# Position bias by a float16 compare on VectorE, sums written by head, placing and high parts on ScalarE

## The chip, the cores and the metric

One core of one Trainium2 chip runs the whole program. The metric is the device time of one execution in microseconds (us). The engines are TensorE (PE; PEld is its weight load), VectorE (DVE), ScalarE (ACT), GpSimd (POOL) and SyncE (SP), whose queue issues nearly all DMAs.

## The reference

The program is an attention with a position bias that a small network computes, then a dense mixture in float64 weights, then a routed one. The change is in the bias and in how float64 weights are converted.

```python
pos = np.arange(S)                      # S = 576
psi_rel = np.log1p(np.abs(pos[:, None] - pos[None, :]))
psi_i = np.log1p(np.maximum(pos[:, None], 1.0))
x = (psi_rel / psi_i)[..., None]
h = np.maximum(x @ w1 + b1, 0.0)        # 32 hidden units
bias = h @ w2                           # 8 heads
scores = q @ k^T / 8 + bias             # then softmax, @ v
...
a, b = x @ moe_w1, x @ moe_w2           # x: [2304, 512]
x = (a * b @ moe_w3) @ moe_w_out
...
out = second mixture: one of 8 experts per row
```

The bias of a query i and a distance d is piecewise linear: unit h counts where w1 log1p(d) + b1 log1p(i) is positive. So for each distance and unit there is a mask over the queries, and the bias is a product of masks with coefficients.

## The kernel before, in words

`build` runs four parts: `p0` (position bias, and the product w3 @ w_out that folds two weights into one), `p1` (attention), `p2` (first mixture), `p3` (second mixture). The order of the instructions on each engine is the order in which the program is written.

`p0` goes through nine groups `gg` of 64 distances. 128 partitions hold 4 distances times 32 units, so a group has 16 masks of up to 576 queries (L239 to L250; the last three groups need 512, 384 and 256 columns only, by `COLS`). For each of up to five query tiles `t` of 128 (or 64) queries, TensorE multiplies each mask by three bfloat16 parts of the coefficients `mv` (L324): 48 products of 64 columns into one PSUM tile `pb`, of which there are three. 39 such tiles are made in all. The 64 columns hold two sums, one that is divided by log1p(i) and one that is not, for 4 distances and 8 heads. `evac` then has ScalarE scale the first sum into `tmp` (L255) and VectorE add the second, writing the distance table `ds` (L266). `flush` writes a finished table of 128 distances to `dsym` in DRAM (L208) and, mirrored by POOL into buffers `md` (L222), a second time (L225). There are two `md` buffers, which the pieces of w3 @ w_out use as well (L236, L237).

Coefficients: POOL multiplies and splits them into three parts `p3a` (L142, L144, L155), and VectorE places them with four instructions, one for each distance of the four, zeros elsewhere (`place`, L151). The constant sum's parts `p3c` are placed once for each of two buffers.

Masks of the next group are made while a group's products run. `NACT` says how many of 16 ScalarE makes, as a steep sigmoid (L248); the others VectorE makes with a compare (L250).

Woven in are 24 conversions of float64 weights (`conv_steps`, L79): the high word is scaled (L93 or, on ScalarE, L91; `CVE` names the engine of each), three VectorE steps put in the low bits (L97, L98, L99), POOL makes the high part in TensorE's rounded format (L193) and subtracts it to give the low part (L194). SP loads the next piece (L169) when a piece has been converted. `mixed` is the list in which a group's masks on VectorE, conversion steps and placing are sorted by their place in the group; it is cut into as many pieces as there are tiles, and after each piece stands the add of the tile before.

`p2_operands` converts 16 pieces of the first mixture's weights with the same steps, the scaling on VectorE (`mul`, L642), then a cast to the high part on ScalarE (L661) and POOL's subtraction (L659).

## Time and profile before

| | |
|---|---|
| Time, median of 3 runs | 1084.18 us (1083.52 to 1087.68) |
| Span of the profiled execution, first to last instruction | 1082.5 us |
| Busy share of the span | PE 93%, PEld 83%, DVE 74%, ACT 63%, POOL 41% |
| First product of the attention's scores | 157.09 us |
| Busy from 0 to 157 us | PE 105.98, DVE 138.76, ACT 101.83, POOL 107.57 us |

The profile shows one execution of the program. The span is the time from its first to its last instruction; the runs' times include what lies around it. A busy share is an average over parts with different limits, so the stretch in which a change lies is read by itself. DVE, ACT, POOL, PE, SP are the engines' names in the rows; L12 is line 12 of the kernel before; `a<-b,c` says which tile is written and which are read.

### The profile page before, as it was taken

What the parts mean: (1) busy time and instruction counts of PE and PEld (TensorE: products, weight loads), DVE (VectorE), ACT (ScalarE), POOL (GpSimd) and SP (SyncE); (2) the same over time, 40 slices, a digit from 0 to 9 for tenths busy, and PEclk for the clock granted to TensorE, in tenths of its full rate; (3) what the DMA queues carried; (4) which work ended last, traced back from release to release, by engine and by line L of the source; (5) the groups of instructions that cost most, each with busy time, mean ns of one, the idle gap of its engine ahead of it and who ended that gap; (6) DMA issues with size and microseconds to landing.
All of it is one profiled execution on the core that took longest, in us unless ns stands there. A gap on an engine that the chain in (4) does not pass through costs nothing.

```text
span 1082.5 us, 21989 instructions
## 1 busy us (share of the span) xinstructions
PE 1005.4 (93%) x8118; PEld 898.7 (83%) x8118; DVE 799.3 (74%) x1447; ACT 677.5 (63%) x1263; POOL 442.2 (41%) x503
## 2 busy tenths in 40 slices
PE   4587789999999999989999999999979999999995
PEld 3566677888888888789999999999978888888884
DVE  8987988999999999999612221222487999989995
ACT  7766556898989888734422222222125888888884
POOL 5766857888888878445300000000033112111220
PEclk9899999999999999989999999999989999999998
DMA  5689765533353432144010000000223326411273
GB/s 170 148 220 240 181 200 163 162 117 109 116 167 112 120 104 83 58 137 146 31 40 10 11 21 21 21 10 11 105 108 120 115 68 213 156 40 40 71 251 96
DMA packets 62419, 116.69 MB, mean 108 GB/s; under 512 B 14495, under 2 KB 33439, under 8 KB 62048
## 3 DMA queue, kind: packets, MB, share of 16 engines
q1 hardware_dynamic: 58496, 104.14, 31.4%
q0 software_dynamic: 3520, 10.75, 3.0%
q8 instruction: 67, 1.10, 0.4%
q14 instruction: 48, 0.39, 0.1%
q10 hardware_dynamic: 288, 0.30, 0.1%
HBM read 155.83 MB, written 25.15 MB: 167 GB/s over the span
## 4 chain that ended last, share of the span: by engine, by line
PE 49%; issue 15%; DMA 11%; DVE 8%; ACT 1%; POOL 0%; POOLq 0%; DVEq 0%; ACTq 0%
PE ab L694 15%; DMA out<-or,sci 10%; PE sc L463 8%; PE o L763 8%; PE pv L549 6%; PE tr L500 5%; PE pv L544 3%; DMA raw<-in_w 1%; PE pv L493 1%; DVE cva L98 1%; PE pv L232 1%; DVE cva L99 1%; DVE cva L97 1%; DVE t L470 1%; DVE cva L93 1%
## 5 line engine op out<-in xcount | busy, mean ns | idle before, releaser
L489 POOL TENSOR_SCALAR e<-e,su 128x576 f32<-128x576 f32 x144 | 114.9, 802 | 58.4 <-DVE su L485 44.8
L740 DVE TENSOR_TENSOR g<-ab,asb 128x256 f32<-128x256 f32 x72 | 30.4, 422 | 143.3 <-ACT asb L739 143.1
L470 DVE CUSTOM_DVE_ANT_0 t<-sc,nb 128x576 f32<-128x576 f32 x144 | 108.4, 753 | 14.4 <-PE sc L463 11.7
L479 ACT ACTIVATE e<-t,mn 128x576 f32<-128x576 f32 x144 | 112.2, 779 | 6.6 <-DVE mn L470 5.1
L324 PE MATMUL pb<-mv,mask 128*128 128x64 bf16 (+1 forms) x1872 | 70.9, 202 | 42.1 <-DVE ds L266 30.5
L1310 POOL DMA_INDIRECT out<-or,sci x21 | 24.8, 1181 | 204.5 <-ACT or L1309 194.8
L324 PEld LDWEIGHTS <-mask 128*128 128x128 bf16 (+1 forms) x1872 | 66.8, 107 | 50.0 <-issue 41.6
L530 DVE TENSOR_TENSOR etl<-tr,eth 128x512 fp32r<-128x512 f32 x144 | 98.5, 684 | 7.4 <-ACT eth L521 4.3
L463 PE MATMUL sc<-kh,qs 128*128 128x288 f32 x320 | 97.6, 322 | 4.5 <-DVE ds L266 4.5
L521 ACT CAST eth<-tr 128x512 fp32r<-128x512 f32 x144 | 83.7, 582 | 28.4 <-PE tr L500 26.3
L935 POOL DMA_INDIRECT xh<-x2r,gi x1 | 1.4, 1354 | 243.8 <-DMA w1r<-in_w1e 243.8
L1207 DVE TENSOR_TENSOR w1l<-w1r,w1h 128x1024 fp32r<-128x1024 f32 x80 | 92.6, 1221 | 5.1 <-ACT w1h L1206 5.1
L694 PE MATMUL ab<-xh,wh 128*128 128x256 f32 x576 | 94.8, 287 | 0.5 <-DVE g L740 0.5
L1258 DVE TENSOR_TENSOR w2l<-w2r,w2h 128x1024 fp32r<-128x1024 f32 x80 | 92.6, 1220 | 2.7
L694 PE MATMUL ab<-xh,wl 128*128 128x256 f32 x576 | 93.5, 285 | 0.4 <-POOL wl L659 0.4
L694 PE MATMUL ab<-xl,wh 128*128 128x256 f32 x576 | 93.4, 285 | 0.0
L463 PE MATMUL sc<-kl,qs 128*128 128x288 f32 x320 | 89.8, 296 | 0.0
L500 PE MATMUL tr<-k_ident,e 128*128 128x128 f32 x576 | 86.4, 273 | 3.1 <-DVE etl L530 3.1
L463 PEld LDWEIGHTS sc<-kh,qs 128*128 128x128 f32 x320 | 60.6, 189 | 30.9 <-issue 11.6
L1206 ACT CAST w1h<-w1r 128x1024 fp32r<-128x1024 f32 x84 | 82.1, 1069 | 0.0
L694 PEld LDWEIGHTS ab<-xh,wh 128*128 128x128 f32 x576 | 80.0, 193 | 1.1 <-DVE g L740 0.8
L694 PEld LDWEIGHTS ab<-xh,wl 128*128 128x128 f32 x576 | 80.2, 193 | 0.6 <-POOL wl L659 0.6
(304 smaller groups left out, 2864.9 us busy)
## 6 DMA issues: line engine op xcount, KB each, us to landing
w1r<-in_w1e SPq DMA_DIRECT2D x84, 512.0 KB
w2r<-in_w2e SPq DMA_DIRECT2D x80, 512.0 KB
q<-in_qd SPq DMA_DIRECT2D x16, 576.0 KB
k<-in_kd SPq DMA_DIRECT2D x16, 576.0 KB
w<-in_w3t SPq DMA_DIRECT2D x16, 512.0 KB
raw<-in_w SPq DMA_DIRECT2D x16, 512.0 KB
nb<-dsym SPq DMA_DIRECT2D x7, 1152.0 KB
dsym<-ds SPq DMA_DIRECT2D x14, 512.0 KB
```

What stands on the lines that cost most here:

```text
L324: nc.tensor.matmul(out=pb[:n, s], lhsT=m_[:, s % 8, P * t:P * t + n], rhs=mv[:, k, s], start=(k == 0), stop=(k == 2))
L463: nc.tensor.matmul(out=sc[:, f, 0:288], lhsT=l, rhs=r, start=(n == 0), stop=(n == len(lst) - 1))
L470: nc.vector.tensor_tensor_reduce(out=t_.rearrange("p (f k) -> p f k", f=2), in0=sc[:, :, 0:288], in1=pre.nb[h % 2][:, tt, :].rearrange("p ...
L479: nc.scalar.activation(out=e, in_=t_, func=AF.Exp, scale=-1.0, bias=mn, accum_out=su[:, i % 2:i % 2 + 1])
L489: nc.gpsimd.tensor_scalar(out=e, in0=e, scalar1=su[:, i % 2:i % 2 + 1], scalar2=1.0, op0=ALU.mult, op1=ALU.mult)
L500: nc.tensor.transpose(pt[:, kb, :], e[:, P * kb:P * kb + P], ident)
L521: nc.scalar.copy(out=dh, in_=src)
L530: nc.vector.tensor_tensor(out=dl, in0=src, in1=dh.bitcast(F32), op=ALU.subtract)
L694: nc.tensor.matmul(out=p[:, a], lhsT=w[f][:, a, k, :], rhs=x[:, k, :], start=(k == 0 and n == 0), stop=(k == KD - 1 and n == 2))
L763: nc.tensor.matmul(out=o[:, a, 0:c1 - c0], lhsT=g[:, sl], rhs=w[:, f, c0:c1], start=(f == 0 and n == 0), stop=(f == KF - 1 and n == 2))
L1207: eng.tensor_tensor(out=w1l[:, k], in0=w1r[:, k], in1=w1h[:, k].bitcast(F32), op=ALU.subtract)
L1258: nc.vector.tensor_tensor(out=w2l[:, sl], in0=w2r[:, sl], in1=w2h[:, sl].bitcast(F32), op=ALU.subtract)
```

## The change

Masks: all 144 are made on VectorE by one compare. Its input is no longer a float32 row of -b1 log1p(i) but the query's number itself in float16 (`qi`), times the sign `sg` of -b1, and the threshold is, for each distance and unit, sg times (exp(w1 log1p(d) / -b1) - 1), made once at the start by short operations and one exponential on ScalarE. `NACT`, the steep sigmoid and ScalarE's masks go.

Sums: `mv` and `pb` are laid out by head, so that `ds` gets runs of 32 distances of one head (forward for query tiles 0 and 1, backward for 2 to 4) in place of single words 128 apart. A mask product now writes its 64 columns in runs of 4 words.

Placing (`place`) goes from VectorE to ScalarE, all first scalings of conversions go to ScalarE (6 of `p0`'s 24 and all 16 of `p2`'s were elsewhere), and `p0`'s high parts go from POOL to ScalarE. At the start, both placings and all 16 masks of the first group come one after the other.

```diff
@@ conv_steps
-            if eng == "A":
-                nc.scalar.activation(out=f, in_=src, func=AF.Copy, scale=2.0 ** -112)
-            else:
-                (nc.vector if eng == "V" else nc.gpsimd).tensor_scalar(out=f, in0=src, scalar1=2.0 ** -112, scalar2=1.0, op0=ALU.mult, op1=ALU.mult)
+            lambda: nc.scalar.activation(out=f, in_=hi.bitcast(F32), func=AF.Copy, scale=2.0 ** -112),
@@ p0
-            nbP = T(c, [P, S], F32, "nbP")
+            qi = T(c, [P, S], F16, "qi")
-            mvs = [T(c, [P, 3, 16, 2, 4, H], BF16, f"mv{r}") for r in range(2)]
+            mvs = [T(c, [P, 3, 16, 2, H, 4], BF16, f"mv{r}") for r in range(2)]
-            v.tensor_scalar(out=nbP, in0=nbP, scalar1=b1c, scalar2=-1.0, op0=ALU.mult, op1=ALU.mult)
-            v.tensor_scalar(out=wL, in0=L4, scalar1=w1c, scalar2=None, op0=ALU.mult)
-            v.tensor_scalar(out=wS, in0=wL, scalar1=STEEP, scalar2=None, op0=ALU.mult)
+            v.tensor_scalar(out=nb, in0=b1c, scalar1=-1.0, scalar2=None, op0=ALU.mult)
...
+            v.tensor_scalar(out=th, in0=L4, scalar1=rb, scalar2=7.0, op0=ALU.mult, op1=ALU.min)
+            v.tensor_scalar(out=qi, in0=qi, scalar1=sg, scalar2=None, op0=ALU.mult)
+            v.tensor_scalar(out=th, in0=th, scalar1=-80.0, scalar2=None, op0=ALU.max)
+            nc.scalar.activation(out=th, in_=th, func=AF.Exp)
+            v.tensor_scalar(out=th, in0=th, scalar1=-1.0, scalar2=sg, op0=ALU.add, op1=ALU.mult)
@@ place
-                    eng.tensor_scalar(out=mvs[r][:, :, :, a, g, :], in0=src, scalar1=blk[:, g:g + 1], scalar2=1.0, op0=ALU.mult, op1=ALU.mult)
+                    nc.scalar.activation(out=mvs[r][:, :, :, a, :, g], in_=src, func=AF.Copy, scale=blk[:, g:g + 1])
@@ conv
-                    gp.tensor_scalar(out=hi, in0=t_, scalar1=1.0, scalar2=1.0, op0=ALU.mult, op1=ALU.mult)
+                    nc.scalar.copy(out=hi, in_=t_)
@@ mask
-                if act:
-                    nc.scalar.activation(out=o, in_=x, func=AF.Sigmoid, scale=-STEEP, bias=wS[:, dq:dq + 1])
-                else:
-                    v.tensor_scalar(out=o, in0=x, scalar1=wL[:, dq:dq + 1], scalar2=None, op0=ALU.is_lt)
+                v.tensor_scalar(out=o, in0=x, scalar1=th[:, dq:dq + 1], scalar2=None, op0=ALU.is_lt)
@@ evac
-                nc.scalar.activation(out=tmp[:n], in_=pb[:n, :, 0], func=AF.Copy, scale=ivp[:n, t:t + 1])
+                nc.scalar.activation(out=tmp[:n], in_=pb[:n, :, 0].rearrange("p b h s g -> p b h (s g)"), func=AF.Copy, scale=ivp[:n, t:t + 1])
-                              [[d.ap[0][0], n], [4 * sg, 16], [sg, 4], [128, H]])
+                              [[d.ap[0][0], n], [32 * sg, 2], [128, H], [sg, 32]])
-                    v.tensor_tensor(out=dst, in0=pb[:n, :, 1], in1=tmp[:n], op=ALU.add)
+                    v.tensor_tensor(out=dst, in0=pb[:n, :, 1].rearrange("p b h s g -> p b h (s g)"), in1=tmp[:n], op=ALU.add)
@@ the groups
-            for q in range(0, 16, 2):
-                mask(0, q, False)
-                mask(0, q + 1, True)
...
+            place(0, 1, c3)
+            pl()
+            for q in range(16):
+                mask(0, q)
...
-                    pb = T(ps, [P, 16, 2, 4, H], F32, "pb")
+                    pb = T(ps, [P, 2, 2, H, 8, 4], F32, "pb")
...
-                            nc.tensor.matmul(out=pb[:n, s], lhsT=m_[:, s % 8, P * t:P * t + n], rhs=mv[:, k, s], start=(k == 0), stop=(k == 2))
+                            nc.tensor.matmul(out=pb[:n, s // 8, :, :, s % 8], lhsT=m_[:, s % 8, P * t:P * t + n], rhs=mv[:, k, s], start=(k == 0), stop=(k == 2))
-                    for x in bga[len(bga) * ti // (nt - 1):len(bga) * (ti + 1) // (nt - 1)]:
-                        x()
@@ mul (first mixture)
-                t_, steps = self.conv_steps(c, raws.pop(divmod(n, 2)), "cv", "V", bufs=2)
+                t_, steps = self.conv_steps(c, raws.pop(divmod(n, 2)), "cv", bufs=2)
```

What this moves is seen in the second group of distances, from the add of its first tile on. VectorE before (L266 is the add, L250 a mask, L97 to L99 a conversion, L151 the placing):

```order
L266 TENSOR_TENSOR ds_41_296<-pb_527,tmp_638 128x64x8
L99 SCALAR_TENSOR_TENSOR w3ta_583<-w_48_371,w3ta_583 128x512
L250 TENSOR_SCALAR mask_712<-nbP_106,wL_114 128x576
L97 TENSOR_SCALAR w3ta_649<-w3ta_649 128x512
L266 TENSOR_TENSOR ds_46_366<-pb_589,tmp_710 64x64x8
L98 SCALAR_TENSOR_TENSOR w3ta_649<-w_53_438,w3ta_649 128x512
L151 TENSOR_SCALAR mv_14_112<-p3a_520,ivb_107 128x48x8 x4
L99 SCALAR_TENSOR_TENSOR w3ta_649<-w_53_438,w3ta_649 128x512
L266 TENSOR_TENSOR ds_52_433<-pb_661,tmp_782 128x64x8
```

VectorE in the changed kernel, from the same add to the third (L264 is the add there, L248 a mask, L86 to L88 a conversion):

```order
L264 TENSOR_TENSOR ds_41_305<-pb_536,tmp_647 128x2x8x32
L248 TENSOR_SCALAR mask_720<-qi_106,th_114 128x576
L87 SCALAR_TENSOR_TENSOR w3ta_590<-w_48_379,w3ta_590 128x512
L248 TENSOR_SCALAR mask_720<-qi_106,th_114 128x576 x2
L88 SCALAR_TENSOR_TENSOR w3ta_590<-w_48_379,w3ta_590 128x512
L248 TENSOR_SCALAR mask_720<-qi_106,th_114 128x576
L264 TENSOR_TENSOR ds_47_372<-pb_598,tmp_718 64x2x8x32
L248 TENSOR_SCALAR mask_720<-qi_106,th_114 128x576 x2
L86 TENSOR_SCALAR w3ta_658<-w3ta_658 128x512
L248 TENSOR_SCALAR mask_720<-qi_106,th_114 128x576 x2
L87 SCALAR_TENSOR_TENSOR w3ta_658<-w_53_446,w3ta_658 128x512
L264 TENSOR_TENSOR ds_52_440<-pb_669,tmp_784 128x2x8x32
```

The four placings have left VectorE, masks stand between nearly all steps, and the conversions keep their steps.

ScalarE before, in the same group (L255 is the scaled sum, L248 a mask, L91 a scaling):

```order
L255 ACTIVATE tmp_638<-pb_527,ivb_107 128x512
L248 ACTIVATE mask_579<-nbP_106,wS_115 128x576 x4
L255 ACTIVATE tmp_710<-pb_589,ivb_107 64x512
L248 ACTIVATE mask_712<-nbP_106,wS_115 128x576 x3
L91 ACTIVATE w3ta_722<-w_58_504 128x512
L255 ACTIVATE tmp_782<-pb_661,ivb_107 128x512
L248 ACTIVATE mask_712<-nbP_106,wS_115 128x576 x4
L255 ACTIVATE tmp_855<-pb_733,ivb_107 128x512
```

ScalarE in the changed kernel, from the same scaled sum to the same fourth one and a little on (L253 is the scaled sum, L194 the high part, L85 a scaling, L152 the placing):

```order
L253 ACTIVATE tmp_647<-pb_536,ivb_107 128x512
L194 CAST xT_131<-w3ta_517 128x512
L85 ACTIVATE w3ta_658<-w_53_446 128x512
L253 ACTIVATE tmp_718<-pb_598,ivb_107 64x512
L253 ACTIVATE tmp_784<-pb_669,ivb_107 128x512
L194 CAST xT_131<-w3ta_590 128x512
L85 ACTIVATE w3ta_792<-w_58_513 128x512
L253 ACTIVATE tmp_855<-pb_735,ivb_107 128x512
L152 ACTIVATE mv_14_112<-p3a_529,ivb_107 128x48x8 x4
L194 CAST xT_131<-w3ta_658 128x512
L85 ACTIVATE w3ta_866<-w_60_522 128x512
```

The masks are gone; in their place stand high parts, which need VectorE's last conversion step, and the placing, which needs POOL's parts `p3a`.

## Rows read from the trace of the kernel before

**Rows 1.** The timeline of TensorE about the first score product: start, us, instruction, wait before it.

```profile
157.09 0.61 PE L463 MATMUL sc<-kh,qs 128*128 128x288 f32 x1 [4.49 <-DVE ds L266]
```

**Rows 2.** Stretches: us, each engine's busy us (count), granted clock, DMA busy share, GB/s.

```profile
core 0: us, PE busy (x) PEld busy (x) DVE busy (x) ACT busy (x) POOL busy (x), PEclk, DMA share, GB/s
20.00:60.00 40.00, 22.54 (x532) 20.84 (x532) 39.32 (x55) 29.72 (x47) 25.69 (x29) 0.83 0.66 170
60.00:100.00 40.00, 31.80 (x585) 26.84 (x583) 29.93 (x46) 27.25 (x44) 25.26 (x39) 0.96 0.87 228
100.00:157.00 57.00, 43.84 (x759) 37.59 (x758) 54.34 (x77) 30.82 (x57) 44.55 (x53) 0.97 0.73 195
0.00:157.00 157.00, 105.98 (x2016) 91.99 (x2016) 138.76 (x209) 101.83 (x165) 107.57 (x145) 0.93 0.72 195
450.00:480.00 30.00, 25.59 (x161) 21.50 (x162) 27.81 (x41) 13.71 (x27) 15.61 (x10) 0.89 0.34 110
480.00:526.00 46.00, 45.67 (x384) 43.90 (x382) 43.39 (x77) 18.78 (x45) 23.00 (x28) 1.00 0.38 123
```

**Rows 3.** Waits from 0 to 157 us: who waited for whom, us, times, longest.

```profile
PE pb L324 <- DVE ds L266: 30.5, 16, 3.7
...
ACT md L236 <- DMA dsym<-md: 12.3, 2, 8.4
POOL md L222 <- DMA dsym<-md: 11.8, 5, 4.5
...
DVE mv L151 <- POOL p3a L142: 8.2, 3, 4.3
```

**Rows 4.** Timeline: start us, us from first start to last end, instruction.

```profile
4.72 0.94 DVE L250 TENSOR_SCALAR mask<-nbP,wL 128x576 bf16<-128x576 f32 x2
...
28.83 1.56 POOL L194 TENSOR_TENSOR xT<-w3ta,xT 128x512 fp32r<-128x512 f32 x1
...
29.29 1.65 DVE L98 SCALAR_TENSOR_TENSOR w3ta<-w,w3ta 128x512 int32<-128x512 int32 x1
...
63.98 1.01 DVE L151 TENSOR_SCALAR mv<-p3a,ivb 128x384 bf16<-128x384 bf16 x4 [4.35 <-POOL p3a L142]
```

**Rows 5.** Single tiles and lines: count, shortest/median/longest ns, first and last start us, shapes.

```profile
L250 DVE TENSOR_SCALAR mask<-nbP,wL x27: 492/561/1528, 4.7 to 94.1; 128x576 bf16<-128x576 f32 x27
...
L250 DVE TENSOR_SCALAR mask<-nbP,wL x19: 380/507/1498, 106.3 to 142.9; 128x512 bf16<-128x512 f32 x9, 128x384 bf16<-128x384 f32 x7, 128x256 bf16<-128x256 f32 x3
...
L151 DVE TENSOR_SCALAR mv<-p3a,ivb x36: 288/314/1467, 9.0 to 146.3; 128x384 bf16<-128x384 bf16 x36
...
L98 DVE SCALAR_TENSOR_TENSOR w3ta<-w,w3ta x24: 669/742/1751, 13.0 to 152.8; 128x512 int32<-128x512 int32 x24
```

**Rows 6.** Groups by line, 0 to 157 us: count, busy us, mean ns, idle before.

```profile
L248 ACT ACTIVATE mask<-nbP,wS 128x576 bf16<-128x576 f32 (+3 forms) x98 | 63.0, 712 | 0.0
L266 DVE TENSOR_TENSOR ds<-pb,tmp 128x512 f32<-128x512 f32 (+1 forms) x39 | 41.1, 1057 | 4.7 <-ACT tmp L255 4.7
...
L250 DVE TENSOR_SCALAR mask<-nbP,wL 128x576 bf16<-128x576 f32 (+3 forms) x46 | 29.9, 671 | 0.0
...
L98 DVE SCALAR_TENSOR_TENSOR w3ta<-w,w3ta 128x512 int32<-128x512 int32 x24 | 24.3, 1011 | 0.4
...
L151 DVE TENSOR_SCALAR mv<-p3a,ivb 128x384 bf16<-128x384 bf16 x36 | 15.8, 500 | 8.2 <-POOL p3a L142 8.2
...
L193 POOL TENSOR_SCALAR w3h<-w3ta 128x512 fp32r<-128x512 f32 x16 | 12.2, 760 | 9.9 <-DVE w3ta L99 9.9
...
L193 POOL TENSOR_SCALAR xT<-w3ta 128x512 fp32r<-128x512 f32 x8 | 5.7, 709 | 8.5 <-DVE w3ta L99 8.5
...
L93 POOL TENSOR_SCALAR w3ta<-w 128x512 f32<-128x512 f32 x4 | 3.4, 862 | 0.0
```

**Rows 7.** Groups by line: VectorE in the attention (whole span), ScalarE from 440 to 530 us.

```profile
L530 DVE TENSOR_TENSOR etl<-tr,eth 128x512 fp32r<-128x512 f32 x144 | 98.5, 684 | 7.4 <-ACT eth L521 4.3
...
L661 ACT CAST wh<-cva 128x512 fp32r<-128x512 f32 x16 | 9.9, 621 | 27.0 <-DVE cva L99 23.6 <-issue 3.4
```

**Rows 8.** Groups by line and shape, 0 to 157 us: ScalarE's masks of 384 columns.

```profile
L248 ACT ACTIVATE mask<-nbP,wS 128x384 bf16<-128x384 f32 x9 | 4.8, 601 | 0.0
```

More of the change, by code (lines that the diff above doesn't have):

```diff
@@ L12 @@
 BF16 = mybir.dt.bfloat16
+F16 = mybir.dt.float16
 I32 = mybir.dt.int32
@@ L115, in p0 @@
             L4 = T(c, [P, 144], F32, "L4")
-            nbP = T(c, [P, S], F32, "nbP")
+            qi = T(c, [P, S], F16, "qi")
             ivb = T(c, [P, 9], F32, "ivb")
             nc.sync.dma_start(out=small, in_=I["mlp"])
-            nc.scalar.dma_start(out=nbP, in_=I["c_P"])
+            nc.scalar.dma_start(out=qi, in_=I["c_Q"])
             nc.sync.dma_start(out=L4, in_=I["c_L4"])
@@ L158, in coefs @@
                 a3 = split3(al, 16, "a")
-                return lambda: place(v, gg % 2, 0, a3)
+                return lambda: place(gg % 2, 0, a3)
             wf = T(late.xp, [P, KD * NT], F32R, "xT")
@@ L287, in p0 @@
                 wph = list(range(WPH[gg], WPH[gg + 1]))
-                bgv, bga = [], []
-                if gg < 8:
-                    na = NACT[gg]
-                    for q in range(16):
-                        act = (q + 1) * na // 16 > q * na // 16
-                        (bga if act else bgv).append(lambda q=q, act=act: mask(gg + 1, q, act))
+                bg = [lambda q=q: mask(gg + 1, q) for q in range(16)] if gg < 8 else []
                 cs = []
@@ L310, in p0 @@
                     if gg == 0:
-                        items.append((0.35, lambda: place(v, 1, 1, c3)))
+                        items.append((0.35, lambda: place(1, 1, c3)))
                     items.append((FP, pl))
@@ L1499, in layout @@
         "c_L4": c(L4),
-        "c_P": c(np.broadcast_to(pi[None, :], (P, S))),
+        "c_Q": c(np.broadcast_to(np.maximum(pos, 1).astype(np.float16)[None, :], (P, S))),
         "c_invP": ivp,
```

35 lines of the change are left out of this document (16 added, 19 removed).

## The prediction

> **What bounds the kernel now.** I read the stretches first, then the waits, then the groups by line, then single operations. The first product of the attention's scores waits for the last add of the position bias [rows 1], so the stretch from 0 to 157 us, which makes that bias and most of w3 @ w_out, ends where VectorE ends. The reader should see in [rows 2] that VectorE is busy in 138.8 of those 157 us and in 39.3 of the 40 us from 20 to 60, while TensorE has work for 106.0 only, and in [rows 3] that TensorE waits 30.5 us for VectorE's adds. From 60 to 100 VectorE is busy in 29.9 of 40 us: there it waits for POOL's parts of the coefficients (8.2 us in all), and POOL and ScalarE wait for the DMAs that empty the md buffers (11.8 and 12.3 us), with the DMA engines at 0.87. So VectorE sets the pace outside 60 to 100, a chain through POOL and DMA inside it. Later on TensorE is the bound; where the change comes in again (conversions of the first MoE's weights), [rows 2] show TensorE busy in 45.67 of 46 us from 480 on, and idle for 4.4 of 30 us before.
>
> **The change, part by part.** The sum is made on VectorE's time in that stretch, in one execution with a span of 1082.5 us; the median of the runs is 1084.18, 1.7 us above it, and a shift of the stretch's end carries over to it one for one. Costs go from start to start, since neighbours overlap.
>
> *a. Masks.* VectorE makes 46 of 144 now, from float32. Two of 576 columns take 0.94 us [rows 4], the last of them 0.50 (the shortest is 0.492, [rows 5]), so 0.44 each; the 19 narrower ones go down to 0.380, which is 0.32 from start to start, and I take 0.38. 27 x 0.44 + 19 x 0.38 = 19.1 us. Afterwards it makes all 144, float16 in and bfloat16 out. The nearest row is the placing, also 16 bits in and out with a scalar per partition: 384 elements, four in 1.01 us with 0.29 for the last [rows 4, 5], 0.24 each. 576 elements are 192 more; float32 masks grow by 0.35 ns per element between 256 and 576 (0.380 to 0.492), so by at most 0.07. I take 0.29, and 0.25 for the 48 narrower ones: 96 x 0.29 + 48 x 0.25 = 39.8. Net +20.7 us. Ends: 0.20 for each, +10; the float32 prices for all, 96 x 0.44 + 48 x 0.38 = 60.5, +41. The Trainium skill ("VectorE: DVE Perf Modes", section "The TRN2 errata — SBUF-src ops pay a fixed extra latency per instruction") has 58 cycles and a quarter of the elements at 0.96 GHz for 16-bit data, an estimate of 0.21 us at 576 columns and 28 us for all, by which the sum below would be about 9 us lower. The same formula with half the elements gives 0.36 where the float32 row shows 0.44, so I stay with the rows.
>
> *b. Placing* moves to ScalarE: 44 x 0.24 = -10.6 us on VectorE.
>
> *c. The adds.* 39 of them take 1.06 us now [rows 6], writing each element 128 words from the last. By head they write runs of 32. The nearest row is the subtraction in the attention, which also reads PSUM and writes one run: 0.684 us for 512 elements [rows 7]. 39 x (1.06 - 0.68) = -14.8. I take that; the other end is 0, because 23 of the 39 write their runs backwards, which no row shows.
>
> *d. Thresholds.* 11 short operations in place of 3; none of the 8 more should take the 0.32 us of a 256-column mask; at 0.17 each, +1.4. The masks start some 2 us later, but now ScalarE makes half of the first 16 at 0.71 us each [rows 6], and 16 x 0.29 is 4.6: the start costs nothing.
>
> *e.* Two scalings leave VectorE, at a mask's 0.44: -0.9. **Sum of a to e: -4.2 us.**
>
> *f. Blocked time.* VectorE's operations lengthen while POOL works: the middle step of a conversion, 0.669 us alone [rows 5], lasted 1.65 beside POOL's subtraction [rows 4]. Mean less shortest, times count [rows 5, 6]: masks 46 x 0.671 - 27 x 0.492 - 19 x 0.42 = 9.6 us; (0.42 lies between the two widths' shortest); placing 36 x 0.212 = 7.6; that step 24 x 0.342 = 8.2; in all 25.4. POOL loses 24 high parts (12.2 + 5.7 us) and 4 scalings (3.4) [rows 6], 21.3 of its 107.6 us, a fifth, which would take 5.1 off. As more masks can be hit, I take -4. Ends: -13 (half of it goes) and +13 (each of 144 masks loses 0.21 us, as 46 do now: 30.2, against 17.2 for masks and placing).
>
> *g. Waiting for POOL's coefficients* (8.2 us, [rows 3]) leaves VectorE for ScalarE, which now places. Behind it stand the next scaled sum and the next high part; VectorE runs on for a tile's work, about 3 us, and then waits for that sum. Half comes back: -4. Ends -8 and 0.
>
> *ScalarE* loses 98 masks (63.0 us, [rows 6]) and gains 44 placings at the 0.60 us of its 384-wide mask [rows 8] (26.5), 24 high parts and 6 scalings at 0.62, like the cast in [rows 7] (18.6): 101.8 - 63.0 + 45.1 = 84 us of the stretch. It has room; placings at twice that would bring it to 110. The mask products' scattered writes to PSUM (runs of 4 words) cost nothing as long as TensorE has some 40 us free; without that cover, each of 39 tiles could take 1 us longer before it showed.
>
> *The first MoE.* 16 scalings go from VectorE to ScalarE, between the cast of one piece and the copy that frees TensorE's accumulator. TensorE is full from 480 on, ScalarE busy in 18.78 of 46 us: 0. Ends -2 (from 450 to 480) and +3.
>
> **What is left of it.** From 60 to 100, a quarter of the stretch, VectorE isn't the bound, so of a to f, -8.2, I count three quarters, -6.2; with g -10.2. 1084.2 - 10.2 = **1074.0 us**.
>
> **Rivals.** *1, slower: masks and POOL exclude one another.* One mechanism: a mask that starts while POOL holds the path to memory waits for POOL to end. 98 masks move from ScalarE, whose rows show no such spread, to VectorE, whose do. For it: masks of 0.492 that took up to 1.528 [rows 5]. Against it: POOL has a fifth less to do. If each mask loses today's 0.21 us, f is +13 and the sum +8.8, with VectorE the bound everywhere: **1093 us**. The point from which it decides: a to e and g give 8.2 us, so masks may lose (17.2 + 8.2) / 144 = 0.18 us each; above that the kernel is slower. The Trainium skill has this as a rule ("Advanced Engine Details and Errata", section "Mode Summary"): VectorE's second SBUF port is shared with GpSimd, and the two block one another. By that rule the trace agrees, with 0.669 us grown to 1.65.
>
> *2, no change: the chain through POOL and DMA.* md buffers, rows written and weight loads stay as they are. If VectorE's gain counts only from 20 to 60, it is 10.2 x 39.3 / 109 = 3.7 us (109 is what VectorE is busy outside 60 to 100): **1080.5**. For it: the DMA engines at 0.87 and the md waits; against it: from 100 on VectorE is busy in 54.3 of 57 us.
>
> *3, the change doesn't do what it says:* the compare gets no faster with float16. Then a is +41, a to f +12.1, three quarters of it and g +5: **1089**.
>
> *4, more than forecast:* masks at 0.20 and half the blocked time gone, a to f -28, about -24 with g and what the other engines leave: **1060**.
>
> **How the numbers follow.** A measurement of this kernel tells about 0.5%, 5.4 us, from no change. Forecast 0.50 (its own range 1064 to 1080), rival 1 0.15, rival 2 0.22, rival 3 0.05, rival 4 0.08. Faster: 0.47 of the forecast, rival 4 and a little of rival 2, 0.57. Same: the rest of rival 2 and of the forecast and the mild end of rival 3, 0.25. Slower: 0.18. The range that leaves out 2 in 10 goes from 1058 (rival 4) to 1093 (rival 1).
>
> **What would show it.** The first score product, at 157.09 now, comes at about 147. Masks of 576 columns: shortest near 0.35 us, mean under 0.55. Adds at 0.68, or two kinds of them if backward runs are slow. The middle conversion step's mean falls from 1.01 towards 0.67 if POOL's relief counts, and rises by rival 1. ScalarE's placings last near 0.6 us, and it, not VectorE, waits for p3a. I would be wrong if masks lose over 0.18 us each, if TensorE comes to wait for ScalarE's placing, or if the time from the first score product to the end, 925.4 us now, moves by over 3 us.

## The result, and the profile after the change

| | before | after |
|---|---|---|
| Time, median of 4 runs | 1084.76 us (1083.52 to 1087.68) | 1099.03 us (1093.66 to 1100.97) |
| Ratio to before, 95% interval | 1 | 1.0117 (1.0088 to 1.0147) |
| Span of the profiled execution | 1082.5 us | 1098.1 us |
| First score product at | 157.09 us | 169.04 us |
| From it to the end of the span | 925.4 us | 929.1 us |

The change makes the kernel slower by 1.2%. The forecast was 1074.0 us in a range from 1058 to 1093; the result lies 6 us above that range. Of the 15.6 us by which the span grew, 12.0 lie before the first score product, where the forecast wanted 10 the other way.

The timeline of TensorE about that product, after:

```profile
169.04 0.40 PE L451 MATMUL sc<-kh,qs 128*128 128x288 f32 x1 [1.72 <-DVE ds L264]
```

The stretches, after (the columns of [rows 2]; the last line goes to the first score product):

```profile
20.00:60.00 40.00, 22.40 (x520) 21.10 (x517) 37.25 (x65) 25.56 (x39) 19.18 (x21) 0.74 0.59 157
60.00:100.00 40.00, 29.89 (x594) 25.64 (x590) 33.99 (x69) 20.81 (x32) 20.69 (x28) 0.91 0.92 231
100.00:157.00 57.00, 39.98 (x625) 34.14 (x622) 36.75 (x81) 26.98 (x41) 31.83 (x44) 0.85 0.63 168
0.00:169.00 169.00, 108.02 (x2016) 94.89 (x2016) 131.87 (x269) 94.86 (x141) 84.05 (x118) 0.87 0.68 181
```

From 100 to 157 us VectorE was busy for 54.34 us before ([rows 2]) and is busy for 36.75 now. Up to the first score product it does 131.9 us of work in place of 138.8, so the work did shrink, by 6.9 us (the sum of a to f was 8.2). But it stands idle for 169.0 - 131.9 = 37.1 us in place of 157.1 - 138.8 = 18.3. **All of the loss is idle time of VectorE**: 18.8 more idle, 6.9 less work, 12 in all. The waits from 0 to 157 us say where it comes from:

```profile
PE pb L314 <- ACT mv L152: 45.6, 8, 13.8
POOL w3l L195 <- ACT w3h L194: 25.5, 5, 9.2
DVE ds L264 <- ACT tmp L253: 20.1, 8, 7.7
POOL xT L195 <- ACT xT L194: 18.5, 6, 7.9
ACT md L237 <- DMA dsym<-md: 15.2, 2, 9.6
...
ACT md L237 <- PE pv L233: 10.7, 2, 5.8
PE pb L314 <- DVE ds L264: 9.4, 7, 2.4
```

TensorE's wait for VectorE's adds fell from 30.5 us ([rows 3]) to 9.4; in its place TensorE waits 45.6 us for the placing on ScalarE (13.8 of them for the first one, where it waited 10.2 for VectorE's before), GpSimd 44.0 for the high parts, VectorE 20.1 for ScalarE's scaled sums. TensorE's first product, before and after:

```profile
10.23 0.96 PE L324 MATMUL pb<-mv,mask 128*128 128x64 bf16 x15 [10.23 <-DVE mv L151]
```

```profile
13.84 9.44 PE L314 MATMUL pb<-mv,mask 128*128 128x64 bf16 x240 [13.84 <-ACT mv L152]
```

ScalarE is busy for only 94.9 of 169 us. What holds it stands in its timeline: it takes its work in order, and the placing has its turn behind copies that wait for a transfer.

```profile
107.85 0.59 ACT L237 COPY md<-pv 128x512 f32<-128x512 f32 x1 [9.56 <-DMA dsym<-md]
108.33 0.69 ACT L253 ACTIVATE tmp<-pb,ivb 128x512 f32<-128x512 f32 x1
108.91 3.55 ACT L152 ACTIVATE mv<-p3a,ivb 128x384 bf16<-128x384 bf16 x4
...
142.85 0.59 ACT L237 COPY md<-pv 128x512 f32<-128x512 f32 x1 [5.64 <-DMA dsym<-md]
143.33 0.69 ACT L253 ACTIVATE tmp<-pb,ivb 128x512 f32<-128x512 f32 x1
143.91 3.54 ACT L152 ACTIVATE mv<-p3a,ivb 128x384 bf16<-128x384 bf16 x4
```

TensorE, in the same execution, starts on the first of these placings:

```profile
112.51 2.72 PE L314 MATMUL pb<-mv,mask 128*128 128x64 bf16 x48 [8.35 <-ACT mv L152]
```

and that stretch by itself (the columns of [rows 2]):

```profile
112.51:115.20 2.69, 2.69 (x49) 2.69 (x49) 1.61 (x2) 2.60 (x5) 2.24 (x2) 0.50 0.58 184
```

The granted clock is 0.50 there, the lower of TensorE's two levels (1.2 GHz), after 8.35 us in which TensorE waited. At 1.00 the same 48 products take 1.57 us (a line of them stands with e1 below), so this wait cost TensorE 1.15 us more than its length. Up to the first score product the mean granted clock is 0.87, where it was 0.93 ([rows 2]).

GpSimd's third part of those coefficients ends at 103.03, 5.9 us before the placing starts. The copy waits for an md buffer, which GpSimd's mirrored rows share with it. Before, the same copy waited nearly as long (12.3 us in two waits, [rows 3]; 15.2 now), but behind it stood scaled sums, as now, and masks of the next group, for which nobody waited yet, in place of the placing.

The single operations, after (count, shortest/median/longest ns, as in [rows 5]), and three groups by line, as in [rows 6]:

```profile
L248 DVE TENSOR_SCALAR mask<-qi,th x144: 273/359/1709, 5.4 to 156.4; 128x576 bf16<-128x576 f16 x96, 128x512 bf16<-128x512 f16 x16, 128x384 bf16<-128x384 f16 x16, 128x256 bf16<-128x256 f16 x16
...
L152 ACT ACTIVATE mv<-p3a,ivb x36: 1046/1082/1167, 10.3 to 160.8; 128x384 bf16<-128x384 bf16 x36
...
L264 DVE TENSOR_TENSOR ds<-pb,tmp x39: 669/679/693, 17.3 to 168.3; 128x512 f32<-128x512 f32 x30, 64x512 f32<-64x512 f32 x9
```

```profile
L248 DVE TENSOR_SCALAR mask<-qi,th 128x576 bf16<-128x576 f16 (+3 forms) x144 | 58.3, 450 | 1.5 <-PE pb L314 1.5
L264 DVE TENSOR_TENSOR ds<-pb,tmp 128x512 f32<-128x512 f32 (+1 forms) x39 | 26.6, 681 | 24.7 <-ACT tmp L253 23.8 <-DMA dsym<-ds 0.7
...
L86 DVE TENSOR_SCALAR w3ta<-w3ta 128x512 int32<-128x512 int32 x24 | 13.8, 574 | 7.0 <-ACT w3ta L85 7.0
```

The adds take 0.68 us, forwards and backwards alike. A placing on ScalarE takes 1.09 on average, not 0.60. And ahead of the adds VectorE waits 23.8 us for ScalarE (4.7 before, [rows 6]), ahead of a conversion's second step 7.0 for the scaling on ScalarE. Of these three waits one (1.4 us) is for a scaling that moved; the other two scalings were ScalarE's before too, and come later now.

### The profile page after: what moved, and what is told of

It reads as the page before. It is cut to its first block, busy times and chain, and to the rows that moved or that the text cites. A ratio compares the mean times of both kernels' runs of the same rounds, so it can differ in the third digit from the quotient of the medians.

```text
span 1098.1 us, 22012 instructions
## 1 busy us (share of the span) xinstructions
PE 1007.3 (92%) x8118; PEld 900.5 (82%) x8118; DVE 783.6 (71%) x1491; ACT 678.2 (62%) x1254; POOL 414.9 (38%) x475
## 4 chain that ended last, share of the span: by engine, by line
PE 26%; issue 15%; DMA 9%; DVE 4%; POOL 1%; ACT 1%; POOLq 0%; ACTq 0%; DVEq 0%
PE ab L682 17%; DMA out<-or,sci 9%; PE o L751 8%; POOL wl L647 0%; DVE cva L88 0%; DVE cva L87 0%; ACT cva L85 0%; DVE g L728 0%; DVE pts L1124 0%; PE ab L780 0%; DVE cand L955 0%; DVE cand L956 0%; PE ab L801 0%; DVE row L773 0%; DVE oh L958 0%
## 5 line engine op out<-in xcount | busy, mean ns | idle before, releaser
L314 PEld LDWEIGHTS <-mask 128*128 128x128 bf16 (+1 forms) x1872 | 69.0, 109 | 64.4 <-issue 51.6
L467 ACT ACTIVATE e<-t,mn 128x576 f32<-128x576 f32 x144 | 112.1, 779 | 10.2 <-DVE mn L458 8.9
L451 PEld LDWEIGHTS sc<-kh,qs 128*128 128x128 f32 x320 | 60.3, 189 | 27.9 <-DVE mn L458 11.4
```

The source lines that it names most:

```text
L314: nc.tensor.matmul(out=pb[:n, s // 8, :, :, s % 8], lhsT=m_[:, s % 8, P * t:P * t + n], rhs=mv[:, k, s], start=(k == 0), stop=(k == 2))
L451: nc.tensor.matmul(out=sc[:, f, 0:288], lhsT=l, rhs=r, start=(n == 0), stop=(n == len(lst) - 1))
L467: nc.scalar.activation(out=e, in_=t_, func=AF.Exp, scale=-1.0, bias=mn, accum_out=su[:, i % 2:i % 2 + 1])
```

## The experiments

The first score product is the measure here, and whole times stand beside it, each as a ratio to runs of the kernel before that were made with it (their medians go from 1084.5 to 1088.4 us). The product's time is that of one profiled execution. Where the code up to it is the same, it agrees within 1.2 us: 169.0 in the changed kernel and 167.9 in e4, 160.8 in e3 and 160.0 in e12. From there to the end, builds whose later code is the same differ by up to 9 us (920.6 with high parts on GpSimd, 929.4 with the early placing; no run here shows the cause of most of it), so a few microseconds of a whole time say nothing of the bias. VectorE's work and idle time up to that product are from the windows view of each run.

| run | VectorE busy | idle | first score product | whole time to before |
|---|---|---|---|---|
| before | 138.8 | 18.3 | 157.1 | 1 |
| after | 131.9 | 37.1 | 169.0 | 1.0117 |
| e1, e2: runs of 8, on VectorE / ScalarE | 148.6 / 137.8 | 19.2 / 35.1 | 167.8 / 172.9 | 1.0106 / 1.0157 |
| e5: placing in words, on VectorE | 158.7 | 10.8 | 169.5 | 1.0087 |
| e6: placing early | 134.2 | 50.9 | 185.1 | 1.026 |
| e3: high parts on GpSimd | 139.2 | 21.5 | 160.8 | 1.0065 |
| e15: copies in their own buffer | 136.0 | 23.1 | 159.1 | 1.0047 |
| e17: e3 and e15 | 145.1 | 8.4 | 153.6 | 0.9981 |
| e14: before, sums by head, placing in words | 142.1 | 18.5 | 160.5 | 1.0041 |
| e13: before, all masks on VectorE | 166.2 | 6.1 | 172.3 | 1.0114 |
| e9: before, float16 masks, split as it was | 133.7 | 18.0 | 151.7 | 0.9956 |

The expectations name theories by letters. In the first eight, A says that TensorE's wait for ScalarE's placing makes the loss, and A2 that it does so by the placing's place in the queue (and not by its length). B is rival 1: masks and GpSimd block one another. D says that the high parts on ScalarE hold its queue up. In the later ones V says that VectorE's queue sets the time, S that ScalarE's does, and L that the order by head has to be paid somewhere.

### What the order by head costs (e1, e2, e5, e10, e14)

e1 puts the coefficients in runs of 8 again, placed by VectorE, and lets the products write single words; e2 is the same with ScalarE placing (without the last pair of lines).

```diff
-mvs = [T(c, [P, 3, 16, 2, H, 4], BF16, ...)]
+mvs = [T(c, [P, 3, 16, 2, 4, H], BF16, ...)]
-nc.tensor.matmul(out=pb[:n, s // 8, :, :, s % 8], ...)
+nc.tensor.matmul(out=pb[:n, s // 8, :, :, s % 8].rearrange("p a h g -> p a g h"), ...)
-nc.scalar.activation(out=mvs[r][:, :, :, a, :, g], in_=src, func=AF.Copy, scale=blk[:, g:g + 1])
+v.tensor_scalar(out=mvs[r][:, :, :, a, g, :], in0=src, scalar1=blk[:, g:g + 1], ...)
```

> The changed kernel with the placing back on VectorE, written in runs of 8 as before (the mask products then write single words, so that the sums still come out by head). Theory A, that TensorE waits for ScalarE's placing (45.6 us in the changed kernel) and this is the loss: the wait for mv falls under 15 us, VectorE takes 11 us more, the first score product comes at 148 to 156 (169.0 in the changed kernel, 157.1 before) and the time is 1078 to 1087. Theory B, rival 1 of the prediction (masks and POOL block one another): 44 more instructions on VectorE that can be blocked, the first score product stays at 168 or later, 1098 or more.

> The same layout as in the run with the placing on VectorE, but the placing stays on ScalarE, so that only its writes (runs of 8 in place of single 2-byte words) and its length change. If the length of the placing (1.09 us, where I had 0.60) makes the loss: 0.60 each, 2.0 us less in each of 9 groups, up to 16 us back, 1084 to 1090. If it is the place in ScalarE's queue, behind copies that wait for md buffers and for TensorE: 0.60 each, but the wait for mv stays over 30 us and the time is 1093 to 1099.

e1: 1095.2 us, 1.0106 (1.009 to 1.0123). e2: 1102.7 us, 1.0157 (1.0125 to 1.0188). The 48 products of a tile, in e1's timeline of TensorE, in that of the changed kernel and in that of the kernel before, each at a granted clock of 1.00:

```profile
102.15 2.85 PE L314 MATMUL pb<-mv,mask 128*128 128x64 bf16 x48
```

```profile
122.21 1.57 PE L314 MATMUL pb<-mv,mask 128*128 128x64 bf16 x48
```

```profile
110.25 1.57 PE L324 MATMUL pb<-mv,mask 128*128 128x64 bf16 x48
```

Writes to PSUM in runs of 4 words cost nothing, as forecast; single words take 1.8 times as long and make TensorE busy for 136.8 of the first 157 us. That hides what the layout was to win; with the same layout, ScalarE as the placing's engine brings the first score product 5.1 us later than VectorE. Neither run decides between its theories: in e1 the wait for the placing goes, as A has it (0.7 us are left), yet the first score product stays at 167.8; in e2 that wait falls to 16.2 us, under the 30 that the theory of the queue asked for, yet no time comes back. e2 also tells the price of the words: in runs of 8 ScalarE takes 0.61 us, the forecast's 0.60, and 1.09 in single words.

```profile
L152 ACT ACTIVATE mv<-p3a,ivb x36: 603/611/632, 8.3 to 161.0; 128x384 bf16<-128x384 bf16 x36
```

e5 undoes only the engine: VectorE places, in single words.

> The changed kernel with the placing back on VectorE and nothing else undone: it writes single 2-byte words 8 bytes apart, the sums stay by head and the mask products write runs of 4 words. Theory A, the placing on ScalarE makes most of p0's loss: the wait for mv goes, the first score product comes at 155 to 160 (169.0 in the changed kernel, 157.1 before). Theory D, the high parts on ScalarE make it (putting them back on POOL brought 160.8): TensorE's wait moves from mv to VectorE's adds, first score product at 164 or later. Placing on VectorE costs 0.3 us each if the words cost nothing, up to 0.8 if they do, 13 to 35 us on VectorE.

1097.8 us, 1.0087 (1.0066 to 1.0108), first score product at 169.5 as in the changed kernel. TensorE no longer waits for ScalarE's placing (but 13.2 us for VectorE's), and nothing is won: single words take VectorE 0.64 us at the median (0.31 before, [rows 5]), and with these and all the masks it has 158.7 us to do. The time is the one that D named, but VectorE's load explains it without D.

```profile
L152 DVE TENSOR_SCALAR mv<-p3a,ivb x36: 601/636/1735, 8.5 to 158.9; 128x384 bf16<-128x384 bf16 x36
```

e10 is the kernel before with the sums by head alone, the placing as it was and the products reading the coefficients in another order (of its edit, the two lines of the products; the adds change as in the change itself); e14 is the same with a placing in single words on VectorE, read in order.

```diff
-pb = T(ps, [P, 16, 2, 4, H], F32, "pb")
+pb = T(ps, [P, 2, 2, H, 8, 4], F32, "pb")
-nc.tensor.matmul(out=pb[:n, s], ..., rhs=mv[:, k, s], ...)
+nc.tensor.matmul(out=pb[:n, s // 8, :, :, s % 8], ..., rhs=mv[:, k, s].rearrange("p a g h -> p a h g"), ...)
```

> The kernel before, with the sums ordered by head alone: the products write their 64 numbers head by head, reading the coefficients, placed on VectorE in runs of 8 as before, in another order (words 16 bytes apart) in place of a placing in that order. Theory V: the 39 adds fall from 41.2 to 26.6 us, the products keep 1.56 us for 48 of them, and the first score product comes 6 to 12 us before 157.1: 0.99 of before. Theory L (the order by head has to be paid somewhere: 48 us on ScalarE, 15 more on VectorE, or 1.3 us for each 48 products on TensorE): the products that read scattered words take over 2 us for 48, and the first score product does not come before 157.

> The kernel before with the sums by head and the coefficients placed on VectorE in single words, which the products then read in order; masks, scalings and high parts as before. Theory V: the adds give 14.6 us of VectorE's work, the placing takes 15 more (0.60 to 0.64 in place of 0.36 to 0.49 us each, 1.0 for the eight of the constant part): no difference, first score product at 154 to 160. Theory that the sums are a gain by themselves: 147 to 151.

e10: 1213.7 us, 1.1184 (1.1163 to 1.1206): theory L, and by far more than the 2 us that it asked for. Reading words 16 bytes apart takes TensorE 10.97 us for 96 products, 5.5 for 48:

```profile
76.85 10.97 PE L324 MATMUL pb<-mv,mask 128*128 128x64 bf16 x96
```

e14: 1089.9 us, 1.0041 (1.0026 to 1.0056), first score product at 160.5: the adds give 14.6 us (41.1 to 26.5), the placing takes 13.4 (24.9 + 7.0 in place of 15.8 + 2.7, busy). The 46 masks take 5.4 more (35.3 for 29.9), which lies in those that share time with an operation of GpSimd (of 576 columns 0.83 us each, 0.68 before; the others 0.43 and 0.42), and TensorE's first product comes 2.2 us later (12.43). **By itself the order by head gains nothing**: what VectorE saves in the adds it, or another engine, pays in the layout of the coefficients.

### ScalarE's queue (e3, e6, e15, e17)

```diff
@@ e3
-nc.scalar.copy(out=hi, in_=t_)
+gp.tensor_scalar(out=hi, in0=t_, scalar1=1.0, scalar2=1.0, op0=ALU.mult, op1=ALU.mult)
@@ e6
-FM, FP = 0.6, 0.6
+FM, FP = 0.6, 0.05
@@ e15
-wsb = T(pools[1], [P, DM], F32, "md") if pools[1] is st else ...
+wsb = T(pools[1], [P, DM], F32, "wsb", bufs=1) if pools[1] is st else ...
```

> The changed kernel with the high parts of p0's conversions back on POOL. If these casts, which wait for VectorE's last step in the middle of ScalarE's queue, hold up the scaled sums and the placing: 8 us or more back, 1091 or less. If the placing is held up by the copies of w3 @ w_out: 0 to 4 us back, 1095 to 1099. By theory B POOL's 18 us more block the masks: slower, 1103.

> The changed kernel with the placing on ScalarE at the start of a group (at 0.05 of its list in place of 0.6), so that it stands ahead of the copies of w3 @ w_out and of most high parts. Theory A2, the placing's place in the queue makes the wait for mv: that wait falls from 45.6 to under 10 us, first score product at 157 to 161. Theory D: high parts still hold up the scaled sums; the wait for mv falls, but VectorE's wait for the scaled sums grows from 20 us and the first score product stays at 165 or later.

> The changed kernel with one thing else: the copies of w3 @ w_out from the accumulators have a buffer of their own, so that ScalarE no longer waits there for a transfer of mirrored rows (15.2 us in two waits, of which one stood ahead of the placing of a group for which TensorE then waited 8.35 us, another ahead of one with 6.63). Theory S: these two waits go, the first score product comes 6 to 12 us before 169.0. Theory V: VectorE's queue is as full as before, it comes at most 3 us earlier.

> The changed kernel with both edits that shortened ScalarE's queue: copies of w3 @ w_out in a buffer of their own, high parts on GpSimd. If ScalarE's queue (theory S) is all that cost time, and the two are separate delays, 8.3 and 9.9 us add up: first score product at 150 to 153, 0.994 of before. If VectorE's queue (theory V), with all the masks in it, is the floor under both: 157 to 161, within 0.5% of before or slower.

e3: 1091.4 us, 1.0065 (1.0048 to 1.0082), first score product 8.3 us earlier than in the changed kernel: the size that D named, and against B, which had it slower. e6, the placing early in a group's work: 1116.3 us, 1.026 (1.0238 to 1.0282), 16 us later instead of earlier. Its waits from 0 to 175 us:

```profile
PE pb L314 <- DVE ds L264: 49.6, 16, 12.2
ACT mv L152 <- POOL p3a L143: 42.6, 7, 11.5
...
DVE ds L264 <- ACT tmp L253: 36.6, 8, 11.5
```

Now ScalarE stands at the placing and waits for GpSimd's parts, and the sums behind it are late. In that form A2 falls: neither of the two places tried is good, early the placing waits for GpSimd, late it is waited for. e7, which adds e3's and e4's edits to the early placing, shows the same (66.4 us of waiting for p3a):

> Placing early on ScalarE, high parts on POOL, the first mixture's scalings on VectorE; masks and sums as in the changed kernel. By A2 and D together both waits go and VectorE is the bound with the 139 us that it is busy or less: first score product at 146 to 153, time 1072 to 1082. If masks and POOL set the pace after all (theory B): 157 or later, 1084 or more.

1108.8 us, 1.0191 (1.0169 to 1.0212). e15 leaves the place and takes away what blocked the queue: 1091.1 us, 1.0047 (1.0029 to 1.0066), first score product 9.9 us earlier, within theory S. The edit also spares GpSimd a wait of 6.9 us for a copy's transfer, and the kernel before was not run with that buffer, so how much of the 9.9 us it would have gained as well is not shown. e17, with e3's edit as well: 1082.4 us, 0.9981 (0.9969 to 0.9994), first score product 15.5 us earlier than in the changed kernel, of 8.3 + 9.9 that would have added up, and 3.5 earlier than before; that is just past the 150 to 153 of two separate delays. Its stretch to that product:

```profile
0.00:153.50 153.50, 105.27 (x2016) 92.52 (x2016) 145.10 (x269) 82.59 (x117) 98.47 (x141) 0.92 0.74 199
```

VectorE is busy in 145.1 of 153.5 us. So the two edits are nearly separate delays, and together they give back more than the 12.0 us that were lost; what VectorE has to do is the floor that is then reached. Two of e17's waits tell which wait counted:

```profile
PE pb L314 <- ACT mv L152: 28.8, 8, 13.1
...
DVE ds L264 <- ACT tmp L253: 3.8, 4, 1.5
```

TensorE still waits 28.8 us for the placing, 13.1 of them at the start, while VectorE's wait for ScalarE's sums has gone from 23.8 us to 3.8 (by way of 14.1 in e3 and 10.6 in e15). TensorE's wait by itself is not the price; what costs time is the part of it that reaches VectorE. Whether e17 is faster than before can't be told at 0.5%.

### The masks alone (e13, e8)

e13 is the kernel before with all 144 masks as float16 compares on VectorE and nothing else of the change (with the thresholds and the row of the change); e8 is the changed kernel with placing (in words) and the first MoE's scalings on VectorE and the high parts on GpSimd. Of e13's edit:

```diff
-NACT = (14, 14, 10, 12, 11, 7, 9, 13)
+NACT = (0, 0, 0, 0, 0, 0, 0, 0)
...
-mask(0, q + 1, True)
+mask(0, q + 1, False)
```

> The kernel before with all 144 masks as float16 compares on VectorE and nothing else of the change (sums, placing, scalings, high parts as before): the mask part alone. Theory V: VectorE's work before the first score product goes from 160 to about 194 us of records (98 masks more, 34.0 us in the changed kernel), ScalarE's falls by 70; the queue is full from start to end and the first score product comes at 172 to 185, 15 to 28 us later than before: 1.014 to 1.026 of before. Theory S (the placing on ScalarE is what costs, the masks are cheap): the first score product stays within 5 us of 157.1, as ScalarE, which made 98 masks, is empty.

> Masks and sums as in the changed kernel, everything that went to ScalarE undone (placing on VectorE in single words, high parts on POOL, the first mixture's scalings on VectorE; only 6 scalings of p0 stay on ScalarE). It shows what masks and sums are worth by themselves. My terms a, c, d and f of the prediction: VectorE gets 21 more, 15 less, 1 more, 4 less and the placing's words on top, first score product at 152 to 160, time 1079 to 1087; theory B: 165 or later, 1092.

e13: 1098.3 us, 1.0114 (1.0097 to 1.0131), first score product at 172.3, the near end of theory V (the whole time lies under that theory's 1.014); e8: 1097.6 us, 1.0081 (1.0059 to 1.0102), at 174.3, as B had it. In both VectorE is full; e13's stretch:

```profile
0.00:172.00 172.00, 113.93 (x2016) 99.47 (x2016) 165.94 (x316) 42.62 (x67) 104.41 (x145) 0.85 0.69 177
```

The mask part is by itself a loss of 15 us up to the first score product (11.7 of the whole time); ScalarE, which made 98 of them, is busy for 42.6 us. The masks by line in e13 and in e17, where VectorE is full too:

```profile
L263 DVE TENSOR_SCALAR mask<-qi,th 128x576 bf16<-128x576 f16 (+3 forms) x144 | 69.7, 527 | 0.0
```

```profile
L248 DVE TENSOR_SCALAR mask<-qi,th 128x576 bf16<-128x576 f16 (+3 forms) x144 | 74.0, 559 | 0.0
```

A mask costs 0.48 to 0.51 us of VectorE there (69.7 and 74.0 over 144), against the 0.28 that one of 576 columns takes undisturbed. The difference is rival 1's: of e13's 96 masks of 576 columns, the 39 during which GpSimd does nothing take 0.28 us each from start to start, none of them more, and the 57 that share time with one of its operations 0.58 on average. (In e17 it is 37 at 0.28 and 59 at 0.57.) The plainest sight of it is at the start of the changed kernel, in the timeline of VectorE (eleven masks together, four of them by themselves, and the last with those behind it):

```profile
5.37 4.77 DVE L248 TENSOR_SCALAR mask<-qi,th 128x576 bf16<-128x576 f16 x11
...
5.68 0.59 DVE L248 TENSOR_SCALAR mask<-qi,th 128x576 bf16<-128x576 f16 x1
6.19 0.47 DVE L248 TENSOR_SCALAR mask<-qi,th 128x576 bf16<-128x576 f16 x1
6.58 0.59 DVE L248 TENSOR_SCALAR mask<-qi,th 128x576 bf16<-128x576 f16 x1
7.09 0.46 DVE L248 TENSOR_SCALAR mask<-qi,th 128x576 bf16<-128x576 f16 x1
...
9.68 2.13 DVE L248 TENSOR_SCALAR mask<-qi,th 128x576 bf16<-128x576 f16 x7
```

and of GpSimd:

```profile
5.67 0.43 POOL L145 TENSOR_TENSOR resta<-al,p3a 128x128 f32<-128x128 f32 x1
6.19 0.30 POOL L143 TENSOR_SCALAR p3a<-resta 128x128 bf16<-128x128 f32 x1
6.57 0.43 POOL L145 TENSOR_TENSOR resta<-resta,p3a 128x128 f32<-128x128 f32 x1
7.09 0.30 POOL L143 TENSOR_SCALAR p3a<-resta 128x128 bf16<-128x128 f32 x1
```

The masks start within 0.01 us of GpSimd's operations, one for one (nine of its ten from 5.67 to 9.68; one mask comes 0.12 us behind): while GpSimd works (until 9.98) a mask comes each 0.43 us, after it each 0.28.

### The first MoE's scalings (e4, e12)

Both put the first MoE's scalings back on VectorE, e12 with the high parts on GpSimd besides. Of their edit, the line that chooses the engine:

```diff
-t_, steps = self.conv_steps(c, raws.pop(divmod(n, 2)), "cv", bufs=2)
+t_, steps = self.conv_steps(c, raws.pop(divmod(n, 2)), "cv", "V", bufs=2)
```

> The changed kernel with the scalings of the first mixture's 16 pieces back on VectorE. The stretch from the first score product to the end is 3.6 us longer in the changed kernel (929.0 against 925.4 us). If that is the scaling on ScalarE: 3 to 4 us back, 1095 to 1096, with p0 unchanged (first score product at 169). If it is chance: 1099.

> The changed kernel with the high parts back on GpSimd and the first MoE's scalings back on VectorE: the two edits that each gave time when undone alone (first score product 160.8 after 169.0 by the first; attention and MoEs 6 to 10 us shorter by the second). If both effects are real and separate: first score product at 160 to 162, 304 us or less from there to the first MoE product, 618 to 620 after it, in all 1084 to 1088, no gain on before. If the second was only the scatter of the later stages: 1090 or more.

e4: 1088.5 us, 1.0048 (1.0026 to 1.007). e12: 1086.5 us, 1.0013 (1.0 to 1.0026), first score product at 160.0, inside the expectation of two separate effects. The first 66 us from the first MoE product on, of the changed kernel and of e4:

```profile
473.60:539.60 66.00, 60.30 (x475) 56.45 (x475) 50.38 (x86) 32.38 (x72) 27.26 (x30) 0.95 0.38 128
```

```profile
467.80:533.80 66.00, 62.27 (x505) 59.34 (x504) 60.22 (x104) 26.44 (x62) 33.64 (x34) 0.97 0.38 128
```

TensorE has 2.0 us less done in the first, and the size is the same in each build: 60.3 to 60.4 with these scalings on ScalarE (the changed kernel, e3, e17), 62.3 to 62.5 with them on VectorE (before, e4, e12). TensorE's longest wait there, for rows that ScalarE copies (3.2 us against 2.0), is more than half of it. The rest of the 10.5 us between the medians of e4 and of the changed kernel lies where the edit doesn't reach: in the profiles 4.1 of it lie between the first and the last score product (288.0 and 284.0 us), and e3, whose edit isn't there either, has 284.1.

### Versions that keep the split (e9, e11, e16)

e9 is the kernel before with the float16 row and thresholds for all masks, 46 on VectorE and 98 on ScalarE as before (the sigmoid reads the same row). e11 adds e10's sums. e16 is e9 with two more masks of each group on ScalarE.

```diff
@@ e9
-o, x = mss[gg, q // 8][:, q % 8, :], nbP
+o, x = mss[gg, q // 8][:, q % 8, :], qi
-v.tensor_scalar(out=o, in0=x, scalar1=wL[:, dq:dq + 1], ...)
+v.tensor_scalar(out=o, in0=x, scalar1=th[:, dq:dq + 1], ...)
...
@@ e16
-NACT = (14, 14, 10, 12, 11, 7, 9, 13)
+NACT = (16, 16, 12, 14, 13, 9, 11, 15)
```

> The kernel before, with one part of the change: the thresholds and the float16 positions feed all 144 masks, 46 of them on VectorE (float16 compare) and 98 on ScalarE (the same sigmoid, reading the float16 row and the scaled threshold), split as before. Sums, placing, scalings and high parts stay as before. Theory V (VectorE's queue sets the position-bias stretch, and the change refilled it: in the changed kernel the 98 masks that came to VectorE brought 34.0 us, the adds and the placing took 14.6 and 21.2 away): VectorE's 46 masks fall from 30.9 us in all to about 20 (0.45 each, as in the changed kernel), the first score product comes 3 to 8 us before 157.1, the time is 0.995 of before. Theory B (a float16 compare and GpSimd block each other, so that it gains nothing where GpSimd is busy): masks stay at 28 us or more or GpSimd's work grows as much, and the first score product stays within 3 us of 157.1. The start may cost 1.5 to 3 us (two more function tables are loaded than in the changed kernel).

> The two runs above together: masks from the float16 row on both engines, split as before, and sums by head with the coefficients read in another order. Theory V: the two gains add up while VectorE's queue is the limit, VectorE's work in the stretch falls from 160 to about 135 us, first score product at 142 to 150, about 0.987 of before; it is then TensorE's 106 us and the chain through the stored bias that limit it. Theory L: no better than the float16 masks alone, or slower.

> The version with float16 masks on both engines (0.9956 of before), with two more masks of each group on ScalarE, 114 in place of 98. Theory V: 16 masks of about 0.5 us leave VectorE, 8 us, ScalarE gains 12 and stays under VectorE: first score product 2 to 6 us before 151.7, about 0.992 of before. If ScalarE's queue is by now as tight as VectorE's: no gain or up to 4 us later.

e9: 1080.3 us, **0.9956** (0.994 to 0.9972), first score product 5.4 us earlier than before, inside theory V; the whole time alone would not tell, as it moved by less than 0.5%. VectorE's work falls from 138.8 to 133.7 us, with the same 18 idle. Its 46 masks give 3.1 of that (29.9 to 26.8), not the 10 of theory V: 38 of them share time with an operation of GpSimd, and those of 576 columns among these take 0.55 us each. e11: 1211.3 us, 1.1161 (1.1142 to 1.118), by e10's reads. e16: 1074.6 us, **0.9887** (0.987 to 0.9903), the fastest kernel here, but not by theory V: its first score product comes at 151.9, no earlier than e9's, which is what the other reading had, ScalarE's queue as tight as VectorE's. VectorE has 6.9 us less to do (126.8) and waits that much longer (25.1). What e16's profile has beyond e9 lies in the last slot of the second MoE, where TensorE waits for a conversion on ScalarE; e16, then e9:

```profile
1061.04 0.47 PE L1316 MATMUL o<-w2h,hh 128*128 128x512 f32 x1 [2.10 <-ACT w2h L1270]
```

```profile
1063.83 0.49 PE L1316 MATMUL o<-w2h,hh 128*128 128x512 f32 x1 [4.85 <-ACT w2h L1270]
```

No edit here touches that place, and other builds stand at either value (e3, e12 and e17 at 1.9; before, the changed kernel and e6 at 4.3 to 4.6); why e16 has the short one stays open. What the float16 masks bring is e9's 5 us.

## Why the prediction was wrong

**The step that failed is "It has room".** ScalarE's load was counted as busy time, 84 us of 157, and a queue that is half empty was taken for one that answers at once. It takes its work in order: behind two waits for md buffers (15.2 us), two for TensorE's products (10.7) and one for a load (6.2), the placing and the sums that others wait for came late. The kernel before showed the first of these ([rows 3]: 12.3 us), and the prediction read it as a limit on VectorE's gain from 60 to 100 us, not as what the placing would stand behind. It named the sign ("if TensorE comes to wait for ScalarE's placing") and gave it no rival and no price. e17 measures what undoing two of these delays gives: 15.5 of the 22 us between the 147 forecast for the first score product and the 169.0 measured. e3's 8.3 of them undo a part of the change; e15's buffer is new, and what it would have given the kernel before was not measured. In the other 6.5 us VectorE is full: it has 145.1 us of work there in place of the forecast's 130.6 (138.8 - 8.2), 74.0 of it masks that GpSimd blocks.

- *a, masks.* 0.29 us was right for an undisturbed mask (0.28). VectorE's busy time for masks rose by 28.4 us (29.9 to 58.3), not 20.7; in e13, with nearly as much work on GpSimd as before (104.4 us), by 39.8.
- *f, rival 1.* Right as a mechanism, and too cheap by the end taken (-4). Undisturbed, 96 masks at 0.28 and 48 at the forecast's 0.25 come to 38.9 us: a mask loses 0.13 us in the changed kernel (58.3), under the 0.18 that decided, but 0.21 in e13 and 0.24 in e17. The changed kernel was spared mostly because GpSimd had less to do (84 us busy in 169, from 107.6 in 157, of which 21 are the high parts and scalings that left it): with the high parts back on GpSimd the masks take 68.2 us (e3), with only the delays shortened 61.1 (e15). The Trainium skill ("Advanced Engine Details and Errata", section "Mode Summary") has GpSimd's instructions and VectorE's two-port ones block each other at a port that they share. The common start times above fit that rule; that it is this port, no run here shows.
- *b and c, placing and adds.* 18.5 us (busy) left VectorE with the placing, more than the 10.6 counted, since 7.6 of blocked time went with it. The adds: -14.5 for -14.8; backward runs cost nothing. But c was never free: the layout that it needs makes a placing in single words, 1.09 us for 0.60 on ScalarE. The prediction had allowed for twice the 0.60 ("would bring it to 110"), but as busy time.
- *a to f together* came to -6.9 us of work, against -8.2. That the sum is near is in part luck: masks and placing missed by 8 us each, in opposite directions. And it holds only beside the delays: where they are partly gone VectorE has 136.0 us of work (e15), and 145.1 (e17) when the high parts are back on GpSimd as well, 6.3 more than before.
- *g.* The wait for GpSimd's parts did leave VectorE (8.2 us to none) and cost ScalarE 0.8. In its place came 23.8 us ahead of the adds, for ScalarE's sums, where half of 8.2 had been set.
- *d.* "The start costs nothing" was wrong by 3.6 us: the first product comes at 13.84 us after 10.23, behind eight placings of 1.1 us in a row.
- *Scattered writes* in runs of 4: nothing, as forecast. *The first MoE:* 2.2 us (62.46 to 60.30 of 66 us) for a forecast of 0, inside its end of +3. The time from the first score product to the end, a sign of being wrong if it moved by over 3, moved by 3.7; these 2.2 are part of it.
- *Rival 3* (the compare gets no faster): no, 0.28 for 0.44 undisturbed; but blocked, 0.48 and more.

## What to carry to other kernels

An engine that is half idle has room for work that nobody waits for. Before work with a deadline is moved to it, list what will stand ahead of it in that queue and what each of those waits for; an idle gap with a releaser in the waits view is a delay to whatever comes behind it. And a layout that makes one engine's access regular has to be paid by the one that writes it: price the new stride on the operation that gets it before counting the gain.
